# The last row tile of the output in three column pieces, and one expert unit moved from batch 2 to batch 1

## The chip, the cores and the metric

The kernel runs on one core of a Trainium2 chip. The metric is the time of one execution in device microseconds; less is better. A kernel is run several times and the median counts. Besides, one execution is profiled: the profile page and the trace come from it, and its span is the time from the first to the last instruction that the profiler records.

The engines are called as in the profile: PE is TensorE (PEld its weight loads), DVE is VectorE, ACT is ScalarE, POOL is GpSimd, SP is SyncE. SPq, ACTq and POOLq are the transfers that these engines issue.

## What is computed

Attention with a window and some global tokens, and a two-layer expert network on its output. All inputs and the output are float32 (the token indices int64).

```python
# q, k, v: (8, 8, 576, 64); global_idx: 8 sorted tokens
scores = (1 / sqrt(64)) * q @ k^T                      # per batch and head, 576 x 576
mask = |i - j| <= 32, or i is global, or j is global
attn = softmax(where(mask, scores, -1e9)) @ v
x = attn.transpose(0, 2, 1, 3).reshape(4608, 512)      # tokens x (heads * 64)
# w_in: (512, 2048), w_out: (2048, 512)
h = x @ w_in
out = relu(h) ** 2 @ w_out                             # (4608, 512)
```

## The kernel before

**Attention.** The eight batches are worked one after the other. A batch has four head pairs, and a pair has two halves of 288 tokens. For a half, PE computes scores of keys by queries for a few key tiles (`scores`, L627), ACT takes the exponential (`exps`, L636), DVE multiplies with the mask (`masked`, L643), and PE multiplies with the values, with a block of ones beside them so that the sums come along (`outputs`, L670 for the first two batches, L679 for the others). ACT then makes the reciprocals of the sums from a logarithm and an exponential (L702, L703), DVE collects what belongs to the global queries (L720) and writes the normalized output, transposed, into `xT` (L732). The two halves of a pair use the two PSUM tiles named `sc` and `acc`, first for their scores and then for their outputs. At the end of a batch, `scatter` writes the eight global rows into `xT` with eight copies on DVE (L751), whose columns are read from registers.

**Expert network.** The 4608 tokens are cut into 9 chunks of 512. The first layer of a chunk is 16 units (`mm1`): four matmuls of 512 columns on PE (L524), a Relu on ACT (L529), a square on DVE (L530). The second layer of a chunk is 4 row tiles of 128 tokens, each in 4 units (`mm2`): four matmuls of 512 columns on PE (L587) per unit; after the fourth unit DVE copies the row tile out of PSUM (`store`, L564) and SP stores it (L566). PSUM tiles for these come in turn from three banks named `mm` and one named `tr` (`expert_bank`).

**What sets the order.** Each engine works through its instructions in the order in which the program text issues them. Units of the expert network stand in a queue in Python, and `take(n)` issues the next n. A unit of chunk c needs the `xT` of its tokens, and so the batches below. `unit(i, n)` issues one head pair: both halves' scores, exponentials and masks, then `take(n[0])`, the first half's outputs, `take(n[1])`, the second half's outputs, after the last pair of a batch the `scatter`, and then `take(n[2])`. The three numbers stand in `SCHED["b1"]` for batch 1's four pairs and further down for the other batches. At the end of each batch from 2 on, `take(99)` issues what is left.

When batch 1 begins, 25 units are in the queue: the rest of chunk 0, the last 16 of them its second layer. Batch 1 takes 23 (7, 6, 6 and 4), which leaves 2, the last two units of chunk 0's last row tile. Batch 2 adds the 32 units of chunk 1 and takes 7, 8, 8 and 9; what is left at its end is issued by `take(99)`. The batches 3 to 6 take 32 each.

After the first half of a batch's first pair, a small copy on POOL (L930) waits for DVE's L720 and so holds back POOL's loads for the next batch: tokens into a scratch in DRAM (L404), which SP then reads back transposed into `kb` and `qb` (L416), and values into `vb` (L113).

**The end.** The last row tile of the last chunk (`last_rows_out`) is not done in one tile of 512 columns but in two column halves, each with 16 matmuls of 256 columns (L572) into a bank of its own, a copy on DVE and a store. The first half's store is issued by SP, the second's by ACT. After its last store SP runs a list of waits, two semaphores at a time, until every transfer and engine has ended; a barrier of all engines follows.

Of the kernel before, what the change touches and what calls it, by code (L numbers as in the profile page):

```python
# [39 lines left out]
)  # L40
W2 = 440
MB = (0, 456)
SCHED = dict(w8=2, w9=3, w5=3, w6=0, w7=4, wa=4, wb=3, wc=3, g0=1, w0=2, w1=4, w2=2, w3=2, w4=3, w=5, h0=0, h1=1, h4=1, h5=1, h2=1, h3=0, keep=1, b1=((3, 1, 3), (2, 1, 3), (2, 1, 3), (2, 1, 1)), last=((2, 1, 4), (3, 1, 4), (2, 1, 4), (2, 1, 7)))
ONES = 2.0**-7 * (1.0 + 15360.0 / 2**23)


# [1 line left out]
def kernel(  # L48
# [10 lines left out]
    nc = tc.nc  # L59
    B, H, S, D = q.shape  # L60
    NG = global_idx.shape[0]
    dm = H * D
    dff = moe_w_in.shape[1]
    P = 128
# [13 lines left out]
    def sbt(name, shape, dtype, bufs=1, tag=None):  # L78
        return sb.tile(shape, dtype, name=name, tag=(tag or name), bufs=bufs)
# [8 lines left out]
    pool, dve, act = nc.gpsimd, nc.vector, nc.scalar  # L88
# [7 lines left out]
    w_out = sbt("w_out", [P, NFF, dm], FP16)  # L96
# [65 lines left out]
    last = KN[-1] + NG  # L162
# [30 lines left out]
    def keep_warm(n):  # L193
        if n:
            w = pst("tr", [P, 512])
        for _ in range(n):
            nc.tensor.matmul(w, idle[:, 0:P], idle, start=True, stop=True)  # L197
# [8 lines left out]
    def indices():  # L206

        low = g64.bitcast(I32).rearrange("p (g two) -> p g two", two=2)[:, :, 0]
        clamped(g32c, 0, S - 1, low)
        nc.vector.tensor_copy(out=g16, in_=low)  # L210
        edges()
        gb = pst("mm", [P, 512])[:, 0:NG]
        nc.tensor.matmul(gb, ones, g16, start=True, stop=True)
        return gb
# [11 lines left out]
    def one_hots(gb):  # L226
        nc.vector.tensor_copy(out=gbf, in_=gb)
        nc.vector.tensor_tensor(
            out=oh, in0=gbf.unsqueeze(1).to_broadcast((P, NT, NG)),
            in1=tok.unsqueeze(2).to_broadcast((P, NT, NG)), op=ALU.is_equal,  # L230
        )
        nc.vector.tensor_tensor(
            out=ohp, in0=gbf.unsqueeze(1).to_broadcast((P, TJ, NG)),
            in1=tokp.unsqueeze(2).to_broadcast((P, TJ, NG)), op=ALU.is_equal,
        )
# [4 lines left out]
    def mask_natural(half):  # L240
        if 1:
            for t, so, c0, w in WIN[half]:
                for grp in range(4):
                    lo, hi = max(grp * GRP, c0), min(grp * GRP + GTOK, c0 + w)
                    o = MB[half] + so + lo - c0
                    if lo < hi:
                        u = lo - 8 * grp - KT * t + U0
                        nc.vector.tensor_copy(
                            out=mask[:, o : o + hi - lo], in_=ub[t // 4][:, u : u + hi - lo]
                        )  # L250
                    lo, hi = max(grp * GRP + GTOK, c0), min((grp + 1) * GRP, c0 + w)
                    o = MB[half] + so + lo - c0
                    if lo < hi:
                        nc.vector.tensor_copy(
                            out=mask[:, o : o + hi - lo],
                            in_=rows[:, t // 4 : t // 4 + 1].to_broadcast((P, hi - lo)),
                        )

    def mask_globals_matmul(half):
        mg = pst("acc" if half == 0 else "mm", [P, 1, 512])  # L260
        if 1:
            wins = [x for x in WIN[half] if x[3] > 8]
            for i, (t, so, c0, w) in enumerate(wins):
                o = c0 - half * BANKC
                nc.tensor.matmul(
                    mg[0:NG, 0, o : o + w], oh[:, t, :],
                    mask[:, MB[half] + so : MB[half] + so + w],
                    start=(i == 0), stop=(i == len(wins) - 1), skip_group_check=True,
                )
        return mg  # L270
# [161 lines left out]
    def cast_tokens(op, nm, hp):  # L432
        t = nat0[(nm, hp)] = sbt("nat0" + nm, [TP, TJ, P], FP16, bufs=2)
        op(out=t.rearrange("p j (h d) -> p h j d", h=2), in_=st[nm][0:TP, pair(hp)])
# [5 lines left out]
    def clear_value_rows():  # L440
        act.copy(
            out=vb[0][0:NG, :, 0 : 2 * H : 2],
            in_=idle[0:NG].rearrange("p (h d) -> p h d", d=D).unsqueeze(1).to_broadcast((NG, NT, H, D)),
        )
# [42 lines left out]
    def tr_k(i, op=None, tail=None, last=None, tag="mm", then=None):  # L487
        op = op or dve.tensor_copy
        tk, gl = transposed("k", i, tag)
        kt = kts[i % NHP]  # L490
        op(
            out=kt[:, 0:4, 8:P].rearrange("p t (q j) -> p t q j", j=TJ),
            in_=tk[:, 0:80].rearrange("p (t q) j -> p t q j", t=4),
        )
        if then:
            then()
        (tail or op)(
            out=kt[:, 4, 8 : 8 + KN[4]].rearrange("p (q j) -> p q j", j=TJ), in_=tk[:, 80:96]
        )
        (last or op)(out=kt[:, :, 0:NG], in_=gl.unsqueeze(1).to_broadcast((P, NT, NG)))  # L500

    def tr_q(i, op=None, tag="mm"):
        op = op or dve.tensor_copy
        tq, gl = transposed("q", i, tag)
        q4 = qts[i % NHP].rearrange("p (g x) -> p g x", x=GRP)
        op(
            out=q4[:, :, 0:GTOK].rearrange("p g (q j) -> p g q j", j=TJ),
            in_=tq.rearrange("p (g q) j -> p g q j", g=4),
        )
        op(out=q4[:, :, GTOK:GRP], in_=gl.unsqueeze(1).to_broadcast((P, 4, NG)))  # L510

    gts = {}
    banks = {"n": 0}

    def expert_bank():
        banks["n"] += 1
        return pst("tr" if banks["n"] % 4 == 0 else "mm", [P, 512])
# [43 lines left out]
    def store(c, m, cols, po, queue):  # L561
        w = cols.stop - cols.start
        ot = sbt("ot", [P, dm], FP32, bufs=4)
        dve.tensor_copy(out=ot[:, 0:w], in_=po[:, 0:w])  # L564
        r0 = c * TC + m * P
        queue.dma_start(out=out[r0 : r0 + P, cols], in_=ot[:, 0:w])  # L566

    def last_rows_out(c, m):
        for i, cols in enumerate((slice(0, dm // 2), slice(dm // 2, dm))):
            po = expert_bank()  # L570
            for f in range(NFF):
                nc.tensor.matmul(  # L572
                    po[:, 0 : dm // 2], gts[c][:, f, m * P : (m + 1) * P], w_out[:, f, cols],
                    start=(f == 0), stop=(f == NFF - 1),
                )
            store(c, m, cols, po, nc.sync if i == 0 else act)

    def mm2(c, m, part):
        if c == NCH - 1 and m == TC // P - 1:
            if part == 0:  # L580
                last_rows_out(c, m)
            return
        if part == 0:
            po_now[0] = expert_bank() if c else pst("mm", [P, 512])
        po = po_now[0]
        for f in range(part * 4, part * 4 + 4):
            nc.tensor.matmul(  # L587
                po, gts[c][:, f, m * P : (m + 1) * P], w_out[:, f, :],
                start=(f == 0), stop=(f == NFF - 1),
            )  # L590
        if part == 3:
            store(c, m, slice(0, dm), po, nc.sync)
# [170 lines left out]
    clear_value_rows()  # L763
    keep_warm(SCHED["w0"])
    gb = indices()
    fetch_globals()
    one_hots(gb)
    keep_warm(SCHED["w1"])
    mask_natural(0)
    mg = mask_globals_matmul(0)  # L770
    keep_warm(SCHED["w2"])
    cast_tokens(dve.tensor_copy, "k", 0)
# [5 lines left out]
    mg = mask_globals_matmul(1)  # L778
    keep_warm(SCHED["w3"])
    ets = {}  # L780

    def half0(i):
        tag = pair_tag[i % 2]
        ets[i] = exps(0, scores(i, 0, tag, WIN), WIN)
# [7 lines left out]
    cast_tokens(dve.tensor_copy, "q", 1)  # L792
    keep_warm(SCHED["w4"])
    tr_k(1, then=lambda: tr_q(1, act.copy))
    keep_warm(SCHED["w5"])
    tr_k(2, then=lambda: (half0(1), tr_q(2, act.copy)))
# [175 lines left out]
```

The softmax here doesn't subtract the row's maximum and nothing guards it: scores larger than these inputs give would overflow.

## Time and profile before

| | us |
|---|---|
| median of 5 runs | 327.65 |
| lowest and highest of them | 327.48, 327.88 |
| the profiled execution's own time | 328.19 |
| its span | 326.4 |
| PE busy in the span | 317.0 (97%) |
| DVE busy | 226.7 (69%) |
| ACT busy | 214.4 (66%) |
| POOL busy | 110.3 (34%) |

Rows of the profile name the source line, the engine, the operation, what is written and read, partitions x elements, and how often (x16). In the chain of waits each step is followed back from the last instruction to what released it. Rows of the timeline begin with the start and the time taken, both in us; where several instructions are merged, the time reaches from the first start to the last end, and matmuls overlap, so that a group's end lies after the next one's start. What stands in square brackets is the idle time of the engine ahead of the row, and what ended it; "issue" there means that the profile shows nothing that the engine waited for. The granted clock of PE was 1.00 throughout.

### The profile page before, as it was taken

The numbers are of one execution on the slowest core, as the hardware profiler recorded it, in microseconds if no ns is written. First come the engines' busy times: TensorE is split into PE (matmuls) and PEld (weight loads), VectorE is DVE, ScalarE is ACT, GpSimd is POOL, SyncE is SP. The second block draws the span as 40 slices with busy tenths as digits, with TensorE's granted clock in tenths as the row PEclk, the third lists the DMA queues.
The fourth block names the chain that finished last, engine by engine and source line by source line (L and its number), as shares of the span: only waits on it lengthen the run. The fifth ranks groups of instructions, "written<-read, shape, count | busy, mean of one in ns | idle before, by whom it ended". The sixth has DMA issues, their size and how long they took to land.

```text
span 326.4 us, 6920 instructions
## 1 busy us (share of the span) xinstructions
PE 317.0 (97%) x2434; PEld 164.8 (50%) x2434; DVE 226.7 (69%) x674; ACT 214.4 (66%) x418; POOL 110.3 (34%) x148
## 2 busy tenths in 40 slices
PE   8989899979999999999999999999999999999996
PEld 3646675435554455455445554455445544444444
DVE  8596987677868875987598758885888675323421
ACT  6787885569953995499549954995499636404600
POOL 9734743739800870089107800680000000000000
PEclk9999999999999999999999999999999999999999
DMA  8999999989993999499959995999710011011012
GB/s 183 175 204 191 161 190 135 203 140 124 150 128 130 71 126 159 157 86 145 121 158 92 144 148 117 105 135 127 137 65 0 34 55 43 2 70 58 2 53 75
DMA packets 148228, 37.53 MB, mean 115 GB/s; under 512 B 136170, under 2 KB 143714, under 8 KB 148194
## 3 DMA queue, kind: packets, MB, share of 16 engines
q0 software_dynamic: 105168, 17.93, 78.5%
q1 hardware_dynamic: 42880, 19.04, 30.3%
q8 instruction: 19, 0.31, 0.4%
q14 instruction: 15, 0.12, 0.1%
q10 hardware_dynamic: 146, 0.13, 0.1%
HBM read 37.30 MB, written 17.05 MB: 166 GB/s over the span
## 4 chain that ended last, share of the span: by engine, by line
PE 89%; DVE 6%; ACT 3%; issue 1%
PE mm L587 28%; PE mm L524 26%; PE tr L524 9%; PE tr L587 7%; PE sc L679 3%; PE acc L679 3%; PE sc L627 3%; PE mm L543 2%; PE acc L627 2%; PE tr L197 2%; DVE xT L751 1%; ACT et L636 1%; DVE et L643 1%; DVE xT L732 1%; PE mm L470 1%
## 5 line engine op out<-in xcount | busy, mean ns | idle before, releaser
L587 PE MATMUL mm<-w_out,gt 128*128 128x512 f16 x448 | 104.2, 379 | 0.0
L524 PE MATMUL mm<-xT,w_in 128*128 128x512 f16 x384 | 90.5, 379 | 0.0
L587 PEld LDWEIGHTS <-gt 128*128 128x128 f16 x560 | 52.4, 98 | 58.8
L524 PEld LDWEIGHTS <-w_in 128*128 128x128 f16 x512 | 47.5, 98 | 52.8
L529 ACT ACTIVATE rl<-mm 128x512 f16<-128x512 f32 x96 | 54.1, 600 | 25.6 <-PE mm L524 25.5
L530 DVE TENSOR_TENSOR gt<-rl 128x512 f16<-128x512 f16 x128 | 51.2, 423 | 17.0 <-ACT rl L529 15.6
L636 ACT ACTIVATE et<-sc 128x880 f16<-128x880 f32 (+1 forms) x32 | 29.0, 906 | 45.3 <-PE sc L627 43.1
L643 DVE TENSOR_TENSOR et<-et,mask 128x880 f16<-128x880 f16 (+1 forms) x64 | 39.1, 615 | 24.2 <-ACT et L636 24.0
L113 POOL DMA_DIRECT2D vb<-in_v_dram x40 | 41.0, 1582 | 8.4 <-DMA w_in<-in_moe_w_in_dram 6.8
L524 PE MATMUL tr<-xT,w_in 128*128 128x512 f16 x128 | 32.9, 380 | 0.0
L564 DVE COPY ot<-mm 128x512 f32<-128x512 f32 (+1 forms) x29 | 19.7, 680 | 18.1 <-PE mm L587 16.4
L636 ACT ACTIVATE et<-acc 128x880 f16<-128x880 f32 (+1 forms) x32 | 29.1, 910 | 1.0 <-PE acc L627 1.0
L703 ACT ACTIVATE rec<-rec 128x288 f32<-128x288 f32 x64 | 28.3, 443 | 2.0
L732 DVE TENSOR_TENSOR xT<-sc,rec 64x288 f16<-64x288 f32 (+1 forms) x55 | 25.0, 455 | 6.5 <-ACT rec L703 6.1
L732 DVE TENSOR_TENSOR xT<-acc,rec 64x288 f16<-64x288 f32 (+1 forms) x55 | 25.0, 455 | 3.9 <-ACT rec L703 1.1
L404 POOL DMA_DIRECT2D scr_k<-in_k_dram x30 | 26.6, 1110 | 2.8 <-issue 2.8
L679 PEld LDWEIGHTS <-vb 128*128 128x128 f16 x288 | 21.3, 98 | 12.3 <-issue 0.8
L930 POOL COPY pin<-gsh 1x1 f32<-1x1 f32 x5 | 0.9, 177 | 78.0 <-DVE gsh L720 78.0
L702 ACT ACTIVATE rec<-sc 64x288 f32<-64x288 f32 (+1 forms) x55 | 22.3, 406 | 6.7 <-PE sc L679 4.8
L404 POOL DMA_DIRECT2D scr_q<-in_q_dram x24 | 24.8, 1570 | 5.1 <-DMA w_out<-in_moe_w_out_dram 5.1
L587 PE MATMUL tr<-w_out,gt 128*128 128x512 f16 x112 | 25.3, 379 | 0.0
L702 ACT ACTIVATE rec<-acc 64x288 f32<-64x288 f32 (+1 forms) x55 | 22.2, 404 | 2.7 <-PE acc L670 1.8
(147 smaller groups left out, 308.8 us busy)
## 6 DMA issues: line engine op xcount, KB each, us to landing
out_dram<-ot SPq DMA_DIRECT2D x35, 256.0 KB
vb<-in_v_dram POOLq DMA_DIRECT2D x32, 120.0 KB, 11.2
scr_q<-in_q_dram POOLq DMA_DIRECT2D x24, 144.0 KB, 6.1
scr_k<-in_k_dram POOLq DMA_DIRECT2D x24, 120.0 KB, 3.8
w_in<-in_moe_w_in_dram POOLq DMA_DIRECT2D x4, 512.0 KB, 11.5
w_out<-in_moe_w_out_dram POOLq DMA_DIRECT2D x4, 512.0 KB
natk<-in_k_dram POOLq DMA_DIRECT2D x3, 288.0 KB, 6.9
natq<-in_q_dram POOLq DMA_DIRECT2D x3, 288.0 KB, 7.7
```

The source lines that it names most:

```text
L113: pool.dma_start(out=vb[b][NG : NG + KN[x], x, 2 * hs.start : 2 * hs.stop : 2], in_=v[b, hs, x * KT : x * KT + KN[x]].rearrange("h s d -> ...
L404: pool.dma_start(out=scr[(nm, b % 2)][x * pitch + off : x * pitch + off + hi - lo].rearrange("s (h d) -> s h d", d=D), in_=src[nm][b, :, l ...
L524: nc.tensor.matmul(ph, w_in[:, t, u * P : (u + 1) * P], xT[:, t, XOFF + c * TC : XOFF + (c + 1) * TC], start=(t == 0), stop=(t == NDM - 1),)
L529: nc.scalar.activation(out=rl, in_=ph, func=AF.Relu)
L530: nc.vector.tensor_tensor(out=gts[c][:, u, :], in0=rl, in1=rl, op=ALU.mult)
L587: nc.tensor.matmul(po, gts[c][:, f, m * P : (m + 1) * P], w_out[:, f, :], start=(f == 0), stop=(f == NFF - 1),)
L636: act.activation(out=et[:, :, 0:W], in_=sc[:, :, 0:W], func=AF.Exp, bias=0.0, scale=scale)
L643: dve.tensor_tensor(out=et[:, :, 0:W], in0=et[:, :, 0:W], in1=mask[:, MB[half] : MB[half] + W].unsqueeze(1).to_broadcast((P, 2, W)), op=AL ...
L679: nc.tensor.matmul(banks[e][:, o : o + w], vtf[:, t, vo : vo + P], et[:, e, so : so + w], start=(n == 0), stop=(n == nw - 1), skip_group_c ...
L702: act.activation(out=rec[r], in_=av[xs][rs, :, 0:GTOK], func=AF.Ln)
L703: act.activation(out=rec, in_=rec, func=AF.Exp, scale=-1.0)
L732: dve.tensor_tensor(out=xT[r, hp, x0 : x0 + HS].rearrange("p (k x) -> p k x", k=2), in0=av[x][r, :, 0:GTOK], in1=rec[r], op=ALU.mult,)
```

## The change

There are two edits. The last row tile of the output is cut into three column pieces, of 256, 128 and 128 columns, where it had two of 256; the first and the third are stored by SP and the second by ACT. And the last pair of batch 1 takes two units at its end where it took one, so that 24 of the 25 units are issued in batch 1 and one is left for batch 2.

```diff
 SCHED = dict(
 ...
-    b1=((3, 1, 3), (2, 1, 3), (2, 1, 3), (2, 1, 1)),
+    b1=((3, 1, 3), (2, 1, 3), (2, 1, 3), (2, 1, 2)),
 ...
     def last_rows_out(c, m):
-        for i, cols in enumerate((slice(0, dm // 2), slice(dm // 2, dm))):
+        for i, cols in enumerate((slice(0, 256), slice(256, 384), slice(384, dm))):
             po = expert_bank()
             for f in range(NFF):
                 nc.tensor.matmul(
-                    po[:, 0 : dm // 2], gts[c][:, f, m * P : (m + 1) * P], w_out[:, f, cols],
+                    po[:, 0 : cols.stop - cols.start], gts[c][:, f, m * P : (m + 1) * P], w_out[:, f, cols],
                     start=(f == 0), stop=(f == NFF - 1),
                 )
-            store(c, m, cols, po, nc.sync if i == 0 else act)
+            store(c, m, cols, po, act if i == 1 else nc.sync)
```

The order of PE's instructions around the end of batch 1, in groups:

```
before                                   after
12 L670 acc (outputs, batch 1)           12 L670 acc
 4 L587 (chunk 0)                         8 L587 (chunk 0)
 6 L627 sc  (scores, batch 2)             6 L627 sc
 6 L627 acc                               6 L627 acc
 8 L587 (chunk 0)                         4 L587 (chunk 0)
                                          4 L524 (chunk 1)
 6 L679 sc  (outputs, batch 2)            6 L679 sc
 4 L524 (chunk 1)                         4 L524 (chunk 1)
 6 L679 acc                               6 L679 acc
```

From there on each unit of batch 2 stands one place earlier among the pairs, until the flush at the batch's end. The order in the batches 3 to 7 is the same as before up to the last row tile. POOL's instructions are the same; SP has one store more at the end.

More of the change, by code (lines that the diff above doesn't have):

```diff
@@ L42 @@
 MB = (0, 456)
-SCHED = dict(w8=2, w9=3, w5=3, w6=0, w7=4, wa=4, wb=3, wc=3, g0=1, w0=2, w1=4, w2=2, w3=2, w4=3, w=5, h0=0, h1=1, h4=1, h5=1, h2=1, h3=0, keep=1, b1=((3, 1, 3), (2, 1, 3), (2, 1, 3), (2, 1, 1)), last=((2, 1, 4), (3, 1, 4), (2, 1, 4), (2, 1, 7)))
+SCHED = dict(w8=2, w9=3, w5=3, w6=0, w7=4, wa=4, wb=3, wc=3, g0=1, w0=2, w1=4, w2=2, w3=2, w4=3, w=5, h0=0, h1=1, h4=1, h5=1, h2=1, h3=0, keep=1, b1=((3, 1, 3), (2, 1, 3), (2, 1, 3), (2, 1, 2)), last=((2, 1, 4), (3, 1, 4), (2, 1, 4), (2, 1, 7)))
 ONES = 2.0**-7 * (1.0 + 15360.0 / 2**23)
```

## Prediction

> **What bounds the kernel now.** I read the page first, for which engine carries the span.
>
> ```profile
> span 326.4 us, 6920 instructions
> ...
> PE   8989899979999999999999999999999999999996
> ...
> PE 89%; DVE 6%; ACT 3%; issue 1%
> ```
>
> The reader is to see TensorE (PE) at nine tenths in almost every slice and carrying 89% of the chain. Nothing on another engine pays unless it removes PE idle time, PE work, or something after PE's last matmul. So the next view is what PE waited for between 60 and 70 us, where batch 1 gives way to batch 2, then PE's busy time over the rest of the run (the second column is the stretch, the third PE).
>
> ```profile
> PE acc L627 <- issue: 1.6, 1, 1.6
> PE sc L679 <- DVE et L643: 0.5, 1, 0.5
> ```
> ```profile
> 72.00:319.00 247.00, 247.00 (x1553) 121.42 (x1552) 170.40 (x477) 163.01 (x315) 69.75 (x80) 1.00 0.99 99
> ```
>
> From 72 us PE is busy for 247.00 of 247.00 us. The same question from 70 us to the end names no wait that begins after 70. So PE idles at one place only after 60 us, around 65 to 70, and a unit of PE work that is put there comes off the end. The third view is that place in the order of time.
>
> ```profile
> 64.14 1.04 PE L587 MATMUL mm<-w_out,gt 128*128 128x512 f16 x4
> 65.11 0.36 PE L627 MATMUL sc<-qb,kb 64*128 64x160 f16 x6
> 65.12 0.41 ACT L702 ACTIVATE rec<-acc 128x288 f32<-128x288 f32 x1 [1.46 <-PE acc L670]
> ...
> 66.61 0.45 DVE L732 TENSOR_TENSOR xT<-acc,rec 128x288 f16<-128x288 f32 x1
> 67.10 1.66 DVE L751 COPY xT<-gx 128x4 f16 x8
> 67.11 0.37 PE L627 MATMUL acc<-qb,kb 64*128 64x112 f16 x6 [1.64 <-issue]
> ...
> 67.42 1.90 PE L587 MATMUL mm<-w_out,gt 128*128 128x512 f16 x8
> 68.17 0.90 ACT L636 ACTIVATE et<-sc 128x880 f16<-128x880 f32 x1 [2.16 <-PE acc L627]
> ...
> 69.77 0.62 PE L679 MATMUL sc<-et,vb 128*128 128x160 f16 x6 [0.46 <-DVE et L643]
> ```
>
> The second half of batch 2's first scores (67.11) waits for the bank that L732 reads until 67.06. L679 (69.77) waits for the mask L643 (69.10 to 69.72), which stands in VectorE's (DVE's) order behind the eight copies L751 of the scatter, the last of which ends at 68.75. By the start-to-start times of the matmuls, less the time their columns take, the two gaps are 1.80 and 0.62 us: 2.42 us.
>
> ScalarE (ACT) is late here for an odd reason. L702 starts at 65.12, though the last matmul it waits for (L670) ended at 64.21, and L636 at 68.17, though its scores ended at 65.47 and ACT was free from 66.01. In the trace's semaphore records PE's signal comes at 65.10 and 68.14. It lags its matmul by over 0.3 us nowhere else in the run.
>
> **Part 1, the unit.** Batch 1's last pair now takes two units at its end. The four matmuls L587 at 64.14 become eight, the eight at 67.42 become four, and behind those four stands the first unit of chunk 1 (L524), ahead of L679. No instruction is added or removed; later in batch 2 each unit stands one place earlier, and the flush at its end takes one unit instead of two. A unit is four matmuls of 216 ns, 0.86 us.
>
> With ACT's and DVE's times as they stand, PE goes like this. Eight L587 run 64.14 to 65.87, the scores 65.97 to 66.3, a wait to 67.11 (0.8 instead of 1.8 us), scores to 67.4, four L587 to 68.27. The unit L524 reads what the scatter writes, so it waits for L751 until 68.8 and runs to 69.67. L679 is ready at 69.67 and starts at 69.77 as before, since the mask sets it. So at 69.77 PE has done one unit more: **-0.86 us**, if the rest stays dense.
>
> Does it? Queued behind the new wait on PE are L679 and, behind it, L702 on ACT, and L679 was waiting anyway. The Relu of the early unit takes ACT's place from 69.87 to 70.47; L702, at 70.43 before, moves by 0.04. Its square L530 (0.43) now precedes L720 on DVE, so L720 moves from 71.28 to about 71.54, and the copy on GpSimd that releases batch 3's loads with it, 0.26 later. Batch 3's transposed q and k landed by 98.8 and PE used them at 102.41: 3.6 us of slack, of which the change uses 0.26 and 0.86. The scatter at the end of batch 2 ended at 101.84, 1.0 us before the first L524 that reads it; four fewer matmuls stand between, but an output copy (0.69) moves ahead of it on DVE, so about as much slack is left. Later batches keep their order. The other cover is the load of relus: pairs of 7, 8 and 1 first-layer units (batches 3 on) run with no wait on PE, and batch 2 goes from 5, 8, 3 to 6, 8, 2, which is nearer to those.
>
> The bounds of this part are 0.86 and nothing. I take 0.86, because what sets 67.11 and 69.77 is on ACT and DVE and not ahead of PE.
>
> **Part 2, the last row tile.** Two views: the chain, and the timeline of the tail.
>
> ```profile
> 86.92 0.38 PE acc L679 x6
> ...
> 319.67 1.75 PE tr L572 x16
> ```
> ```profile
> 321.25 1.91 PE L572 MATMUL mm<-w_out,gt 128*128 128x256 f16 x16
> 321.45 0.42 DVE L564 COPY ot<-tr 128x256 f32<-128x256 f32 x1 [1.05 <-PE tr L572]
> 323.20 0.42 DVE L564 COPY ot<-mm 128x256 f32<-128x256 f32 x1 [1.32 <-PE mm L572]
> 323.65 0.38 ACTq L566 DMA_DIRECT2D out_dram<-ot  x1
> ```
>
> - Matmuls. 16 of 256 columns become 32 of 128; the columns are the same, 16 weight loads and matmuls are more. A 256-column one takes 1.75/16 = 109 ns. L679 shows narrower ones, each with a weight load of its own: six of 880 columns in 0.38 us, and start to start 49 ns at 112 columns, 59 ns at 136. Between these, 128 columns take 56 ns: 32 x 56 - 1.75 = **+0.04 us**. The upper bound is the load and the matmul one after the other, 98 + 56 = 154 ns: +3.2. I take the L679 row, it has the same load and nearly the width.
> - Copy. 0.69 us for 512 columns and 0.425 for 256 give 1.0 ns a column: 0.295 for 128, **-0.13** (bounds 0 and -0.21, half of 0.425). The middle piece's copy (about 322.35 to 322.65) lies under the last 16 matmuls, and its store on ACT's queue too.
> - Queue. From issue to first packet the SyncE (SP) store of the first half took 0.83 us (321.90 to 322.73), ACT's 0.87 (323.65 to 324.52): **-0.04**.
> - Transfer. First to last packet took 0.83 us for 256 KB and 0.53 for 128 KB, so 64 KB should take 0.38: **-0.15** (bounds 0 and -0.26).
> - Ending. SP sees the last store 0.36 us after its last packet (325.05 to 325.41) and then works through three more steps of 0.06 to 325.61, from where the barrier takes 0.8 to the span's end. The third store has the next semaphore in this list, so one step goes: **-0.06**. SP issues the last store and only then does its other waits, some nine of 0.06 from 323.9 to 324.5, under a transfer that is seen at 325.1.
>
> The sum of part 2 is -0.34 us (from -0.5 to +3.1 by the bounds).
>
> The Trainium skill, "TensorE: Matmul & The Clock Gate", section "Back-to-back issue gap", speaks against the narrow pieces: in a stream where each matmul has its load it gives some 81 ns at 128 columns, and 131 ns at 512. By it the pieces would cost 32 x 81 ns - 1.75 = +0.84 us and part 2 would lose 0.46, an estimate from that page. The trace disagrees with both of its figures (49 and 59 ns around 128 columns, 216 ns at 512), and the measurement decides.
>
> **Sum.** -0.86 - 0.34 = -1.20 us. The profiled execution took 328.19 us with a span of 326.4; its span would be 325.2 and its time 327.0. The five runs have a median of 327.65, 0.54 below it; taken off that: **326.45 us** (-0.37%).
>
> **Rivals.**
> - *The signals are on time in unprofiled runs* (19%). Nothing shows that the late PE signals are in every execution. On time, L702 starts at 64.23 and the scatter ends near 67.85; before then idles 0.7 us at the scores and some 0.3 ahead of L679, while the changed order has no idle at the scores and 0.4 ahead of the unit. Gain 0.55 instead of 0.86: 326.75.
> - *The idle time moves along* (17%). If PE's signal is late because of what PE does next (65.10 is just when PE leaves L587 for L627), four more L587 put it, L702, the scatter and L679 0.86 later, and the unit fills nothing: 327.3. Against it: the second late signal (68.14) falls in the middle of L587, and both come 0.03 to 0.1 us after DMA completions, silent from 64.32 and 67.36, resume (65.05, 68.05). That points to the transfers, which are issued before the changed place.
> - *The end of a store is fixed*, only part 1 counts (6%): 326.8.
> - *The weight loads do not hide in the narrow pieces* (3%), the one that ends slower. Load then matmul, 154 ns, is +3.2 us on PE's last stretch, where nothing covers it; with the other terms (-0.38, -0.86) it is +1.9: 329.6. It makes the whole no gain from 93 ns a matmul, and slower by 0.2% from 114. The 112-column row at 49 ns speaks against it.
> - *Batch 3's inputs come late* (2%): it needs a slip beyond the 2.5 us left, and over 1.9 us more to end slower than before by 0.2%.
>
> **Numbers.** The forecast has 53%: 326.45. The range is 326.2 to 327.3: down by the better bounds of the copy and the store (0.2), up to the idle that moves along. 0.2% (0.65 us) is about what a measurement of this kernel tells from no change. Faster by more: 53 + 19 + 6 = 78%; within: 17%; slower: 5%.
>
> **What would show it.** In the changed profile, part 1 is right if L679's first matmul of batch 2 starts near 69.8 with one L524 group ahead of it, PE's wait at the scores is near 0.8 us, and from 70 us on PE has no wait. It is wrong if that start is near 70.6, or if a new wait stands in batch 2 or at batch 3's start. Part 2 is right if the 32 narrow matmuls take 1.79 us, the last copy 0.3, and some 2.87 us lie between PE's end and the span's end, against 3.25 before (323.16 to 326.41); it is wrong if the groups of 16 take over 1.2 us. A late start of the last store on SP would mean that it was held by something in that queue.

## The result, and the profile after

| | before | after |
|---|---|---|
| median, us | 327.89 (57 runs) | 326.90 (30 runs) |
| lowest and highest, us | 326.89, 329.56 | 326.47, 327.42 |
| the profiled execution's own time, us | 328.19 | 326.73 |
| its span, us | 326.4 | 324.9 |

The ratio is 0.9966 (95%: 0.9957 to 0.9974), so the change takes 0.34% off, which is 327.89 x 0.0034 = 1.1 us (0.9 to 1.4 by the interval). The ratio compares all runs and is not quite the quotient of the two medians, which lie 0.99 us apart. The 57 runs of before begin with the five shown ahead of the prediction, whose median was 327.65. The executions of before lie within 2.7 us, those of after within 1.0 (within 1.8 when after was measured once more, below).

The page of after, the same lines as before the change:

```profile
span 324.9 us, 6956 instructions
...
PE   8989899989999999999999999999999999999996
...
PE 90%; DVE 6%; ACT 2%; issue 1%
```

PE bounds the kernel as it did. Of the 36 instructions more, 32 are the 16 weight loads and 16 matmuls of the narrower pieces. What PE waited for from 60 us to the end (in total, times, longest), and PE's busy time from 72 to 318:

```profile
PE sc L679 <- DVE et L643: 0.5, 1, 0.5
PE mm L524 <- DVE xT L751: 0.4, 1, 0.4
```
```profile
72.00:318.00 246.00, 246.00 (x1549) 121.03 (x1547) 169.75 (x475) 162.27 (x313) 69.70 (x80) 1.00 1.04 99
```

The wait of 1.6 us that stood at the scores (L627) is gone. A new one of 0.4 stands at the early unit (L524), and that at the mask (L643) stayed. From 72 us on PE is dense, as before. The place in the order of time:

```profile
64.11 1.90 PE L587 MATMUL mm<-w_out,gt 128*128 128x512 f16 x8
64.22 0.41 ACT L702 ACTIVATE rec<-acc 128x288 f32<-128x288 f32 x1 [0.59 <-PE acc L670]
...
65.94 0.36 PE L627 MATMUL sc<-qb,kb 64*128 64x160 f16 x6
66.19 1.72 DVE L751 COPY xT<-gx 128x4 f16 x8
66.21 0.37 PE L627 MATMUL acc<-qb,kb 64*128 64x112 f16 x6
...
67.90 0.90 ACT L636 ACTIVATE et<-sc 128x880 f16<-128x880 f32 x1 [2.80 <-PE mm L587]
67.96 1.02 PE L524 MATMUL mm<-xT,w_in 128*128 128x512 f16 x4 [0.41 <-DVE xT L751]
...
69.50 0.62 PE L679 MATMUL sc<-et,vb 128*128 128x160 f16 x6 [0.52 <-DVE et L643]
```

L679 starts at 69.50 (69.77 before), with the unit L524 ahead of it. By start-to-start times PE's two gaps here are 0.58 us, ahead of L524, and 0.68, ahead of L679: 1.26 in place of 2.42. ACT's L702 is on time in this execution (64.22, not 65.12), so the bank that L732 reads is free early and the scores do not wait at all. L636 is still late: its scores ended at 66.3 and it starts at 67.90.

The tail: the chain's last PE steps, then the timeline of the last piece.

```profile
318.53 1.75 PE tr L572 x16
320.27 1.80 PE mm L572 x32
```
```profile
320.11 1.95 PE L572 MATMUL mm<-w_out,gt 128*128 128x128 f16 x32
...
322.10 0.29 DVE L564 COPY ot<-mm 128x128 f32<-128x128 f32 x1 [0.60 <-PE mm L572]
```

The 32 narrow matmuls take 1.80 us, 0.05 more than the 16 wide ones. PE ends at 322.06, the span 2.86 us later (3.25 before).

For the experiments three lengths are read from each profile: where L679 first starts in batch 2; the stretch from there to PE's last matmul; and the tail from there to the span's end. They add up to the span. Before: 69.77 + 253.39 + 3.25 = 326.41. After: 69.50 + 252.56 + 2.86 = 324.92. Each profile is one execution.

### The profile page after: what moved, and what is told of

Its sections match the earlier page's. It is cut to its first block, busy times and chain, and to the rows that moved or that the text cites. A ratio compares the mean times of both kernels' runs of the same rounds, so it can differ in the third digit from the quotient of the medians.

```text
span 324.9 us, 6956 instructions
## 1 busy us (share of the span) xinstructions
PE 316.9 (98%) x2450; PEld 164.8 (51%) x2450; DVE 226.8 (70%) x675; ACT 214.3 (66%) x418; POOL 110.2 (34%) x148
## 4 chain that ended last, share of the span: by engine, by line
PE 90%; DVE 6%; ACT 2%; issue 1%
PE mm L587 30%; PE mm L524 25%; PE tr L524 9%; PE tr L587 7%; PE sc L679 3%; PE acc L679 3%; PE sc L627 3%; PE mm L543 2%; PE acc L627 2%; DVE xT L751 1%; PE tr L197 1%; PE sc L670 1%; PE acc L670 1%; PE mm L470 1%; ACT rec L703 1%
## 5 line engine op out<-in xcount | busy, mean ns | idle before, releaser
L587 PE MATMUL mm<-w_out,gt 128*128 128x512 f16 x448 | 104.4, 379 | 0.0
L524 PE MATMUL mm<-xT,w_in 128*128 128x512 f16 x384 | 90.8, 379 | 0.4 <-DVE xT L751 0.4
L587 PEld LDWEIGHTS <-gt 128*128 128x128 f16 x560 | 52.4, 98 | 58.6
L524 PEld LDWEIGHTS <-w_in 128*128 128x128 f16 x512 | 47.6, 98 | 53.6 <-issue 0.7
L636 ACT ACTIVATE et<-sc 128x880 f16<-128x880 f32 (+1 forms) x32 | 29.0, 907 | 45.6 <-PE sc L627 42.8
L643 DVE TENSOR_TENSOR et<-et,mask 128x880 f16<-128x880 f16 (+1 forms) x64 | 39.1, 616 | 25.1 <-ACT et L636 24.8
L524 PE MATMUL tr<-xT,w_in 128*128 128x512 f16 x128 | 33.0, 380 | 0.0
L564 DVE COPY ot<-mm 128x512 f32<-128x512 f32 (+1 forms) x30 | 19.9, 663 | 17.7 <-PE mm L587 16.3
L636 ACT ACTIVATE et<-acc 128x880 f16<-128x880 f32 (+1 forms) x32 | 29.1, 909 | 1.0 <-PE acc L627 1.0
L732 DVE TENSOR_TENSOR xT<-sc,rec 64x288 f16<-64x288 f32 (+1 forms) x55 | 25.0, 455 | 6.4 <-ACT rec L703 5.9
L732 DVE TENSOR_TENSOR xT<-acc,rec 64x288 f16<-64x288 f32 (+1 forms) x55 | 25.0, 455 | 3.9 <-ACT rec L703 1.1
L679 PEld LDWEIGHTS <-vb 128*128 128x128 f16 x288 | 21.3, 98 | 12.3 <-issue 0.9
L702 ACT ACTIVATE rec<-sc 64x288 f32<-64x288 f32 (+1 forms) x55 | 22.3, 406 | 6.2 <-PE sc L679 4.2
L587 PE MATMUL tr<-w_out,gt 128*128 128x512 f16 x112 | 25.3, 379 | 0.0
L702 ACT ACTIVATE rec<-acc 64x288 f32<-64x288 f32 (+1 forms) x55 | 22.3, 405 | 1.8 <-PE acc L670 1.0
```

Of the source, the lines that this page charges most:

```text
L524: nc.tensor.matmul(ph, w_in[:, t, u * P : (u + 1) * P], xT[:, t, XOFF + c * TC : XOFF + (c + 1) * TC], start=(t == 0), stop=(t == NDM - 1),)
L587: nc.tensor.matmul(po, gts[c][:, f, m * P : (m + 1) * P], w_out[:, f, :], start=(f == 0), stop=(f == NFF - 1),)
L636: act.activation(out=et[:, :, 0:W], in_=sc[:, :, 0:W], func=AF.Exp, bias=0.0, scale=scale)
L643: dve.tensor_tensor(out=et[:, :, 0:W], in0=et[:, :, 0:W], in1=mask[:, MB[half] : MB[half] + W].unsqueeze(1).to_broadcast((P, 2, W)), op=AL ...
L679: nc.tensor.matmul(banks[e][:, o : o + w], vtf[:, t, vo : vo + P], et[:, e, so : so + w], start=(n == 0), stop=(n == nw - 1), skip_group_c ...
L702: act.activation(out=rec[r], in_=av[xs][rs, :, 0:GTOK], func=AF.Ln)
```

## Experiments

My theory was that of the prediction: the unit fills PE idle time that ACT and DVE set, 0.86 us, and the narrow last piece shortens the tail by 0.34. The rivals were that the idle time moves along with PE's work, that PE's signals (the semaphore updates by which it tells the other engines that a matmul is done) are on time in most executions, which makes part 1 worth less, and that the end of a store is fixed. Each ratio below is to the kernel before measured beside that kernel, with its 95% interval; times are compared by these ratios, since the kernel before moved too: its median was 327.02 us beside the first four kernels, 327.11 beside the two units more, the halves on SP, the four pieces and the moved gathers (on another chip), and 327.79 beside the other four.

### The two parts one at a time, and extra work in two places

**Pieces only** (the kernel after, with batch 1's last pair as before):

```diff
-b1=(..., (2, 1, 2))
+b1=(..., (2, 1, 1))
```

> Only the last row tile is changed (256, 128, 128), batch 1's last pair takes one unit as before. If part 2 is worth what the tail of the changed profile shows, the stretch from PE's last matmul to the span's end is 2.87 us against 3.25 before, and the time falls by 0.34 us (ratio about 0.999). If the changed kernel's gain lies in the tail alone, the time falls by 1.0 to 1.1 us (0.9967).

Measured: 326.67 us, 0.9992 (0.9983 to 1.0001). Tail 2.87.

**Unit only** (the kernel before, with that pair as after):

```diff
-b1=(..., (2, 1, 1))
+b1=(..., (2, 1, 2))
```

> Only the unit is moved, the last row tile stays in two halves. If the unit fills idle time of PE at the start of batch 2, the time falls by 0.55 us (PE's signals on time) to 0.86 us (late as in the profile of before): ratio 0.9974 to 0.9983. If the idle time moves along, the time stays (1.000). The tail of 3.25 us should be as before.

Measured: 326.44 us, 0.9977 (0.9967 to 0.9986). Tail 3.25.

The two alone give -0.08% and -0.23%, both together -0.34%: they add up within their intervals. That of pieces only just reaches no change, so its time alone does not show a gain. Its profile does: the tail belongs to the pieces alone, 2.87 with them, 3.25 without.

In both of these profiles L702 came on time (64.23 and 64.16), and so did L636, which was late in the profiles of before and after. So they show part 1 with signals on time. The timeline of pieces only:

```profile
65.50 0.90 ACT L636 ACTIVATE et<-sc 128x880 f16<-128x880 f32 x1 [0.38 <-issue]
66.22 0.37 PE L627 MATMUL acc<-qb,kb 64*128 64x112 f16 x6 [0.77 <-DVE xT L732]
...
68.50 0.62 PE L679 MATMUL sc<-et,vb 128*128 128x160 f16 x6
```

and of unit only:

```profile
66.29 0.90 ACT L636 ACTIVATE et<-sc 128x880 f16<-128x880 f32 x1 [1.24 <-PE sc L627]
67.91 1.02 PE L524 MATMUL mm<-xT,w_in 128*128 128x512 f16 x4 [0.42 <-DVE xT L751]
68.77 0.55 PE L679 MATMUL sc<-et,vb 128*128 128x160 f16 x6
```

With the unit PE no longer idles 0.77 us at the scores, but 0.42 at L524. L679 comes 4.61 us after L702 (68.77 - 64.16) and without it 4.27 (68.50 - 64.23): 0.34 later, with one unit of 0.86 more done. On time, part 1 is worth 0.86 - 0.34 = 0.52 us. Between the profiles of before and after, both with late signals, L679 comes 0.27 earlier, and the stretch behind it is 0.83 shorter though it holds 0.05 more of narrow matmuls: 0.27 + 0.83 + 0.05 = 1.15 us. This is not the unit's worth alone, since L702 was late as well in the profile of before and on time in that of after.

**Four matmuls in the idle place** (before, with four matmuls of 512 columns on zeros, into the bank `tr`, that nothing reads; they stand at the end of batch 1):

```diff
             gather(0)
+            keep_warm(4)
```

> The kernel before with four matmuls of 512 columns more, on a tile of zeros and into a bank that nobody reads, at the place where the change puts its unit (end of batch 1). They are 0.86 us of work that computes nothing. If PE's time there is idle and the rest does not depend on when the scores of batch 2 come, the time does not change (within 0.2 us). If the idle time moves along with PE, it grows by 0.86 us (1.0026). In between if the scores that come later hold up ACT and DVE.

Measured: 327.33 us, 1.0013 (0.9997 to 1.0029). In its timeline:

```profile
64.95 1.03 PE L197 MATMUL tr<-idle 128*128 128x512 f16 x4
...
68.63 0.62 PE L679 MATMUL sc<-et,vb 128*128 128x160 f16 x6 [0.25 <-DVE et L643]
```

L679 comes 4.45 us after L702 (64.18), against 4.27 in pieces only: 0.86 us of PE work costs 0.18 here. The stretch (253.34) and the tail (3.25) are those of before. "The idle time moves along" asked for L679 to come 0.86 later. (L702 and L636 were on time in this execution.) The ratio alone could not have told this: its interval holds both 0 and 0.26% (0.86 us).

**The same four matmuls where PE is dense** (after the last pair of batch 4):

```diff
             unit(...)
+            if b == 4 and hp == 3:
+                keep_warm(4)
```

> The same four matmuls, but after the last pair of batch 4, where the profile shows no wait of PE. Both theories expect 0.86 us more (1.0026): this is the price of four matmuls where PE has no idle time, against which the run with the fill at the end of batch 1 is read.

Measured: 329.92 us, 1.0084 (1.0071 to 1.0097): 2.7 us, not 0.86. The view of PE's waits says why:

```profile
PE tr L197 <- DVE ot L564: 1.6, 1, 1.6
```

The added matmuls write the bank `tr`, which DVE was still copying out (L564), so PE waited as well. The stretch is 256.11, 2.72 longer than the 253.39 of before: 0.86 of work, a gap of 1.72 at this wait, and one of 0.18 at 206.7. So the run tells the price of work in a dense place only after its wait is taken off. It does show that nothing hides a delay of PE there.

### More of the same, and the rest of the tail

**Two units more** (the kernel after, with three units behind that pair):

```diff
-b1=(..., (2, 1, 2))
+b1=(..., (2, 1, 3))
```

> The changed kernel with one unit more at the end of batch 1 (three where before has one), so that none of chunk 0 is left for batch 2 and its first pair begins with two units of chunk 1, which read what the scatter writes. If the scatter and the mask behind it set the start of the outputs, PE now waits for the scatter ahead of two units, 1.73 us, and the outputs start about 0.4 to 0.9 us later than in the changed kernel with one unit more done: the time is that of the changed kernel within 0.4 us. If more units at this place go on filling idle time, it falls by a further 0.5 us or more.

Measured: 326.54 us, 0.9982 (0.9968 to 0.9997). No gain over one unit is shown (0.9966, and the intervals overlap).

```profile
67.63 1.89 PE L524 MATMUL mm<-xT,w_in 128*128 128x512 f16 x8 [0.60 <-DVE xT L751]
```

The wait for the scatter grows to 0.60, and L679 (69.35) comes 5.47 us after L702, where it was 4.61 in unit only: the second unit costs its full 0.86. PE also has new gaps where batch 3 begins, by start-to-start times: 0.12 us at 100.5 more than in unit only, where the scatter ends at 100.75 and the L524 that reads it starts at 100.80; then 0.34 at 102.3 and 0.13 behind it, at the outputs L679, whose mask L643 stands on DVE behind two output copies. There the prediction had counted "about as much slack" for one unit; a second uses it up.

**Both halves stored by SP** (before, the second half's store on SP in place of ACT):

```diff
-store(c, m, cols, po, nc.sync if i == 0 else act)
+store(c, m, cols, po, nc.sync)
```

> The kernel before, with the store of the second half issued by SP in place of ACT. By the packet records, SP's store begins 0.04 us sooner, and nothing else of the tail changes but the order of SP's own waits: 0.0 to -0.1 us. If the queue were what matters in the tail, -0.3 us.

Measured: 327.26 us, 1.0002 (0.9990 to 1.0014). Tail 3.21 against 3.25: 0.04 us, the size that the issue times had given.

**Four pieces** of 256, 128, 64 and 64 columns (the middle two on ACT):

```diff
-slice(0, 256), slice(256, 384), slice(384, dm)
+slice(0, 256), slice(256, 384), slice(384, 448), slice(448, dm)
-store(c, m, cols, po, act if i == 1 else nc.sync)
+store(c, m, cols, po, act if i in (1, 2) else nc.sync)
```

> The changed kernel with its third piece cut again: 256, 128, 64, 64, stored by SP, ACT, ACT and SP. By the linear rows the last copy takes 0.23 instead of 0.29 us and the last transfer, in packets of 256 B, 0.29 instead of 0.36; 16 matmuls more at about 2.5 ns each add 0.04 us: -0.1 us. If a matmul with its weight load cannot go below some 38 ns (the narrowest with 128 x 128 weights in the trace of before), 32 of 64 columns take 1.22 us instead of 0.93 and the sum is +0.2 us.

Measured: 326.59 us, 0.9976 (0.9962 to 0.9990). Tail 3.11, longer than with three pieces.

```profile
321.00 0.23 DVE L564 COPY ot<-mm 128x64 f32<-128x64 f32 x1 [0.17 <-PE mm L572]
321.46 0.23 DVE L564 COPY ot<-mm 128x64 f32<-128x64 f32 x1 [0.24 <-PE mm L572]
```

The matmuls were no obstacle: those of 64 columns start 29 ns apart. The copy is shorter (0.23 instead of 0.29), and SP sees the last store 1.75 us after PE's end, 0.18 earlier than with three pieces (1.93). But the trace's semaphore records show that this fourth store has the semaphore that comes third in SP's closing list, so that nine more steps follow once it is seen (323.17), until 323.73: 0.56 us. With three pieces two follow.

**A last piece of 64 in three** (the kernel after, with 256, 192 and 64 columns):

```diff
-slice(0, 256), slice(256, 384), slice(384, dm)
+slice(0, 256), slice(256, 448), slice(448, dm)
```

> The changed kernel with pieces of 256, 192 and 64 columns on SP, ACT and SP: the narrow last piece of the run with four pieces, but with three stores, so that the last store keeps the last place in SP's list of waits. If the four pieces lost only by that place, PE's end to the span's end is 2.70 us (2.86 in the changed kernel: copy -0.07, transfer -0.08) and the time 0.13 us lower than the changed kernel's. If a narrow store itself is slower, the tail is 3.0 us or more as with four pieces.

Measured: 327.00 us, 0.9977 (0.9961 to 0.9993). Tail 2.84, hardly better than 2.86: neither the 2.70 nor the 3.0 of the expectation.

```profile
322.77 0.38 ACTq L566 DMA_DIRECT2D out_dram<-ot  x1
```

ACT issues the middle store, now of 192 columns, only at 322.77, and SP sees it at 324.55; the last piece's own signal comes after it, and SP sees that one at 324.72. By the packet records the copy and the transfer of the last piece are shorter, about as expected (from PE's end to its issue 0.30 us, and first to last packet 0.30, where both were 0.36). But its packets (323.95 to 324.25) now overlap those of the middle store (323.65 to 324.13), and from its last packet until SP sees it 0.47 us pass, where it was 0.38, and 0.36 with four pieces, whose last two transfers do not overlap. That the overlap makes it so late fits these rows and was not tested by itself.

### The late signals

**The gathers at another time** (the kernel after; POOL's three indirect transfers, the `gather` that stood at the end of batch 1, are issued in the first pair of batch 2, where the tokens' load now also stands ahead of the global rows'):

```diff
-        elif hp == 3:
-            gather(0)
...
-                globals_to_scratch(b + 1)
-                tokens_to_scratch(b + 1)
+                if b == 2:
+                    tokens_to_scratch(b + 1)
+                    gather(0)
+                    globals_to_scratch(b + 1)
+                else:
+                    globals_to_scratch(b + 1)
+                    tokens_to_scratch(b + 1)
```

> The changed kernel, with the three gathers of POOL that run at 63.5 to 67 us put behind the token loads of batch 3 (some 13 us later). If these gathers make PE's signals late between 64 and 68 us, every PE signal there comes within 0.3 us of its matmul, ACT's exponentials of the first scores start near 66.4 instead of 67.9, and L679 starts near 68.9 instead of 69.5: up to 0.5 us less, unless batch 3's transposed keys come too late. If the small value transfers or the value loads make them late, the late signals stay.

Measured: 326.08 us, 0.9966 (0.9953 to 0.9979), the same ratio as the kernel after over all its runs: the gain of up to 0.5 us did not come. Its profiled execution took 327.16, since the time before batch 2 was 1.3 us longer in it. POOL's gathers and ACT's exponential in its timeline:

```profile
80.86 1.04 POOL L331 DMA_INDIRECT gstk<-in_k_dram,gidx  x1 [0.30 <-issue]
...
83.48 0.97 POOL L331 DMA_INDIRECT gstv<-in_v_dram,gidx  x1 [0.30 <-issue]
```
```profile
67.63 0.90 ACT L636 ACTIVATE et<-sc 128x880 f16<-128x880 f32 x1 [1.24 <-PE sc L627]
```

The scores ended at 67.58, so L636 is on time here. This can't be put down to the moved gathers: of the thirteen profiles with the gathers at their old place (some 63.5 to 67 us), seven have L636 on time too, 0.04 us behind its scores. The other six have it late: by 2.69 us in before, 1.59 in after, 1.56 in after once more, and 1.83, 0.72 and 1.44 in the last piece of 64 in three, the unit from the pair ahead, and both together. Pieces only and halves on SP have the same order of instructions there as before, unit only and four pieces that of after, and all four are on time: what differs is the execution and not the kernel.

The semaphore records show more than PE's signals. In each of the six late profiles the updates of all semaphores, those of DMA completions included, stand still for 0.4 to 0.8 us at a time, five or six times between 63.9 and 68.6 us, while instructions of ACT, DVE and PE that make such updates end; the late L636 starts 0.04 to 0.12 us after the end of such a stretch. In the other eight profiles no such stretch is over 0.38 us. The six have one to three more at the later gathers (near 153 to 156 us in all, near 86 in two), and nowhere else: all lie within the gathers or up to 1.0 us behind them. So in the executions that have them they go with the gathers in time, and in others the same gathers run without any. The run with the moved gathers is of the second kind at all its gathers, so it does not tell whether moving them helps.

**A unit from the pair ahead** (the kernel after, but batch 1's third pair takes one unit less). Batch 1 then takes 23 units as before the change, and no L524 stands ahead of L679, so that PE need not wait there for the scatter:

```diff
-b1=((3, 1, 3), (2, 1, 3), (2, 1, 3), (2, 1, 2))
+b1=((3, 1, 3), (2, 1, 3), (2, 1, 2), (2, 1, 2))
```

> The changed kernel, with the extra unit at the end of batch 1's last pair taken from the end of the pair before it (batch 1 takes 23 units again, and the first pair of batch 2 begins with two units of chunk 0, which do not wait for the scatter). If the chain from the last pair's scores to the mask L643 sets the start of L679, it comes 0.86 us earlier than in the run with the pieces alone: L679 near 67.6 with no wait ahead of an L524, 0.2 to 0.3 us less than the changed kernel. If ACT and DVE do not follow, L679 starts near 68.5 with one unit fewer done and the time is 0.5 to 0.6 us above the changed kernel's.

Measured: 326.61 us, 0.9955 (0.9941 to 0.9969).

```profile
66.43 0.91 ACT L636 ACTIVATE et<-sc 128x880 f16<-128x880 f32 x1 [1.92 <-PE acc L627]
...
68.18 0.65 PE L679 MATMUL sc<-et,vb 128*128 128x160 f16 x6 [0.36 <-DVE et L643]
```

L679 starts at 68.18 where 67.6 was expected: ACT's first exponential was late in this execution too, 0.72 us behind its scores, and the second started 0.6 us after ACT was free.

**This and the 64-column last piece together:**

```diff
-b1=(..., (2, 1, 3), (2, 1, 2))
+b1=(..., (2, 1, 2), (2, 1, 2))
-slice(0, 256), slice(256, 384), slice(384, dm)
+slice(0, 256), slice(256, 448), slice(448, dm)
```

> The two edits together, pieces of 256, 192 and 64 and the unit from the pair before. If both are worth what the theory says, 0.3 to 0.45 us below the changed kernel (ratio to before 0.9950 to 0.9960); if neither, the changed kernel's time.

Measured: 326.40 us, 0.9961 (0.9944 to 0.9977). L679 at 68.76, after an L636 that was 1.44 us late; tail 2.85.

**The kernel after once more**, nothing edited, measured beside the last piece of 64, the unit from the pair ahead, and both together:

> The changed kernel as it is, on the same chip as the three others, for the comparison. Ratio to before 0.9957 to 0.9974 as already measured. Whether PE's signals come late at the start of batch 2 differs from execution to execution, by the profiles so far: if so, L679 starts at 68.8 (on time) or 69.5 (late) and nothing else in the profile differs.

Measured: 326.79 us, 0.9973 (0.9959 to 0.9987). Its profile is that of after again: L679 at 69.53, tail 2.87. The unit from the pair ahead has the best ratio, but 326.61 and 326.79 are 0.18 us apart and the intervals overlap widely; none of these versions is shown to be faster than the kernel after.

## Why the prediction was right, and where it was off

**The whole.** Forecast -0.37%, measured -0.34%. The time of 326.90 is 0.45 above 326.45: 0.24 because the five runs that the forecast started from had their median that much below that of all 57 (327.65, 327.89), and 0.21 because the medians are 0.99 apart and not 1.20. By the ratio the gain is 1.1 us: part 2's 0.34 came out, and part 1 was, if anything, sized a little too high.

**Part 1, -0.86.** The step "with ACT's and DVE's times as they stand" was the weak one. They do not stand: the late signals come and go between executions. The promised wait of 0.8 at the scores did not come in the profile of after, since L702 was on time there; the wait at L524 did (0.58, forecast some 0.5), and behind it PE's gap ahead of L679 was 0.68, with its start at 69.50 and not 69.77. The unit has its 0.86 us in full (the stretch from L679 to PE's end is 0.83 shorter in after, with the narrow matmuls' 0.05 in it). What varies is where L679 starts: 0.34 us later with the unit when the signals are on time, 0.27 earlier between the two profiles of before and after. Part 1 is thus worth 0.52 on time, close to the rival's 0.55, and 1.15 between those two late executions, where a part comes from the L702 that was late in one alone. By the ratio, unit only took off 0.23% of 327 us, 0.75 (0.5 to 1.1 by its interval, which holds the rival's size and the forecast's). So the mechanism was right, a unit that fills idle time of PE; that 0.86 came near the mean is in part luck, because the sum took one execution's lateness for that of all.

**"If the rest stays dense."** It did: 246.00 of 246.00 us. The delay of DVE's and POOL's steps for batch 3 stayed under its cover, and with a second unit that cover was gone.

**Part 2, -0.34.** All five terms came out within 0.02 us:

| term | forecast, us | measured, us |
|---|---|---|
| matmuls | +0.04 | +0.05 (1.80 - 1.75) |
| copy | -0.13 | -0.13 (0.29 - 0.42) |
| issue to first packet | -0.04 | -0.04 (0.83 - 0.87) |
| first to last packet | -0.15 | -0.17 (0.36 - 0.53) |
| last packet to the end of SP's list | -0.06 | -0.05 (0.51 - 0.56) |

The tail is 2.86 (2.87 forecast) against 3.25. SP sees the last store at 323.99, 0.38 after its last packet where it had been 0.36, and two steps follow until 324.12, where there had been three. SP's earlier waits, 322.80 to 323.29, lie under the transfer as worked out.

**The weight loads.** The rival of 154 ns a matmul is refuted: start to start it is 56 ns at 128 columns, which is what the L679 rows gave. Of the Trainium skill's "TensorE: Matmul & The Clock Gate", section "Back-to-back issue gap", the figure of 81 ns for a stream with loads does not hold for these matmuls, each of which has a load; the formula that the section gives for isolated matmuls, N / 2.4 + 2.5, makes 55.8 ns at 128 columns, and that is what the trace shows.

**The other rivals.** "The signals are on time in unprofiled runs" is not refuted: they were on time in eight of fourteen profiles, and its total, 0.55 + 0.34 = 0.89 us, lies at the edge of the interval of 0.9 to 1.4. "The idle time moves along" falls by the four matmuls in the idle place, which PE absorbed but for 0.18 us, by unit only, faster by 0.14 to 0.33%, and by the profile of after, where L702 was not put off by the four L587 more. What it said of the cause, PE's next work, does not fit the records either, in which DMA completions stand still with PE's signals. "The end of a store is fixed" falls by the tail: 2.84 to 2.87 us in all eight profiles with three pieces, 3.25 in the four that have the two halves as before. "Batch 3's inputs late" did not show with one unit.

**Open.** What holds the signals back in some executions, and what part the gathers have in it. How often and how much they are late in runs without a profile is not seen, so the average worth of part 1 can't be worked out from the lines; the 0.75 is from the ratio of the times alone.

## What to carry to other kernels

Where one engine is dense, look for the few places in which it idles and move work there from behind, but find out what ends the next wait: the first unit gained, with a second no further gain showed, and new waits stood here and a batch later. In the tail only the last piece counts, until the store ahead of it overlaps it or its place in the closing list decides: in the two arrangements tried, a last piece of 64 columns brought no more than one of 128. When a trace shows an engine waiting for something that had long ended, look at a second execution before a term of the sum is built on it; and before an edit is called the cure, count how often the trouble is absent without it.

## What the runs showed of the hardware

- In six of fourteen profiles the updates of all semaphores stood still for 0.4 to 0.8 us at a time, only while POOL's indirect gathers ran or up to 1.0 us behind them, and ACT started up to 2.7 us after the matmuls that it waited for; in the other eight the same gathers ran with no stretch over 0.38 us. Why is not known.
- Matmuls with a weight load each start 56 ns apart at 128 columns and 29 ns at 64: down to there no floor was reached.
- A store that SP sees early in its closing list costs 0.06 us for each step that follows: in four pieces 0.56 us in place of 0.13, which is more than the 0.18 us by which SP had seen it sooner.
